# A fused attention and gated-FFN block: wv loaded in four row blocks on two queues, and tile 0's first v matmuls ahead of tile 2's transposes

## The chip, the cores and the metric

The kernel runs on one core of a Trainium2 chip. The metric is the device time of one execution in microseconds; the median of several executions is given. A core has five engines with an instruction stream each: TensorE (PE: matmuls, with the weight loads as PEld), VectorE (DVE), ScalarE (ACT), GpSimd (POOL) and SyncE (SP), which here only issues DMAs. ScalarE can issue DMAs too. An engine's stream is worked through in order, and engines wait for one another and for DMAs through semaphores.

## The reference

The input x has 2048 rows (tokens) of 512. It is normalized, and the output is x plus a linear attention of the result plus a gated FFN of it:

```python
qkv = (x @ wqkv) -> q, k, v              # 32 heads of 16
pq, pk = q @ w_phi, k @ w_phi            # per head
phi = concat(softmax(p), softmax(-p))    # for q and for k
kv, z = phi_k^T v, sum(phi_k)            # over all tokens, per head
o = (phi_q kv) / (phi_q z + 1e-6)
A = o @ wo
B = ((x @ w_gate) * (x @ w_up)) @ w_down # 512 -> 1792 -> 512
out = x + A(layernorm(x)) + B(layernorm(x))
```

All inputs are bf16. v takes the last 512 columns of wqkv; these are wv in the kernel, a 512 x 512 matrix.

## The kernel before

The 2048 tokens are 16 tiles of 128. TensorE contracts over partitions, so it needs the normalized x transposed: xnT holds, for each of the four 128-row blocks c of the 512 features, the 128 tokens of each tile. A projection of one tile into 512 columns is four matmuls of 512 columns, one for each block c, that add up in one bank of PSUM (`proj`); matmul j reads block j of xnT and row block j of the weights.

The instruction order of all five engines is written out by hand (`manual_schedule`): what stands first in the program text for an engine runs first on it. The SyncE DMAs at the top come in the order of the text too.

At the start of the program tiles 0 to 3 of x are treated apart, so that TensorE has work early:

- x tiles 0 and 2 are loaded by SyncE's queue, x tiles 1 and 3 by ScalarE's (`dma_x`, L68 and L69). Behind its two x tiles SyncE's queue issues wv in two halves of two row blocks each (`dma_wv`, L74 to L76, called in L84 and L85), then the first columns of w_gate and w_up (`dma_gu`, L72), w_phi (L87), further columns, the transposed load of the k part of wqkv (wT, L89), and the rest of x and of the weights.
- ScalarE's first instruction is a small Exp (L101), which brings its function table in; then its two x loads, then the sum of tile 1 (L376, tile `junk`, whose accumulated output is `tots[1]`).
- VectorE sums tile 0 (`sum_of`, L373) and makes 512 x - sum of it in two halves (`sub_sum`, L337, tile xn), then does the same subtraction for tile 1, and then sum and subtraction for tile 2 and for tile 3. Scaling by 1/std comes later, since it can be applied to the result of the projection.
- TensorE transposes xn of each tile (`lt`, L202 to L206, four transposes of 128 x 128; tile 0 in two halves) and ScalarE copies the result from PSUM into xnT (L206).
- `first_v(n, js)` (L353) does those of the four v matmuls of tile n that are named in js. Tiles 0 and 1 accumulate into the two kv banks (shown as `kv` in the profile), tiles 2 and 3 into banks of the common pool (`pv`).
- Ahead of all this `warm_up` (L306) runs matmuls on constants, ten at first, and two more of 512 columns between the transposes of tile 1 and tile 2 (L383).

Behind it come the first three units of the FFN (`ffn(3)`, matmuls L274 and L278), the fold of w_phi into wk (`fold`, L217), which reads wT and `bd`, and then a long stretch in which FFN units, k, v and q projections and the attention alternate.

The order around the change, on TensorE: `lt(0)`, `lt(1)`, two warm-ups, `lt(2)`, blocks 0 and 1 of v of tiles 0, 1 and 2, `lt(3)`, blocks 2 and 3 of v of tiles 0, 1 and 2, all of v of tile 3, FFN.

Of the kernel before, what the change touches and what calls it, by code (L numbers as in the profile page):

```python
# [21 lines left out]
def kernel(  # L22
# [12 lines left out]
    nc = tc.nc  # L35
    P = 128
    S, D = A_x.shape[-2], A_x.shape[-1]
# [4 lines left out]
    DC = D // P  # L42
# [15 lines left out]
    wv = wpool.tile([P, DC, D], BF16)  # L58
# [9 lines left out]
    def dma_x(lo, hi, eng=nc.sync):  # L68
        eng.dma_start(out=xall[:, lo:hi, :], in_=x_view[:, lo:hi, :])  # L69
# [1 line left out]
    def dma_cols(eng, w, src, lo, hi, at=0):  # L71
        eng.dma_start(out=w[:, :, lo - at:hi - at], in_=src[:, lo:hi].rearrange("(c p) f -> p c f", p=P))  # L72

    def dma_wv(lo, hi):  # L74
        nc.sync.dma_start(out=wv[:, lo:hi, :],
                          in_=A_wqkv[lo * P:hi * P, 2 * D:3 * D].rearrange("(c p) f -> p c f", p=P))  # L76

    def dma_gu(lo, hi):
        dma_cols(nc.sync, wg, B_w_gate, lo, hi)
        dma_cols(nc.sync, wu, B_w_up, lo, hi)  # L80

    dma_x(0, 1)
    dma_x(2, 3)
    dma_wv(0, 2)  # L84
    dma_wv(2, DC)  # L85
    dma_gu(0, 2 * P)
    nc.sync.dma_start(out=wphi[:], in_=A_w_phi.rearrange("(c h) d f -> (h d) c f", c=DC))  # L87
    dma_gu(2 * P, 5 * P)
# [12 lines left out]
    nc.scalar.activation(out=first[:], in_=ones[:, 0:1], func=AF.Exp, scale=1.0)  # L101
    dma_x(1, 2, nc.scalar)
    dma_x(3, 4, nc.scalar)
    ident = consts.tile([P, P], BF16)
    make_identity(nc, ident[:])
    mhalf = consts.tile([P, GT], F32)
# [38 lines left out]
    def bank(name, dt=F32, n=TT):  # L145
        return ps_s.tile([P, n], dt, name=name, tag="s")
# [55 lines left out]
    def lt(n, lo=0, hi=DC):  # L202
        tp = bank("tp", BF16).rearrange("p (c t) -> p c t", c=DC)
        for c in range(lo, hi):
            nc.tensor.transpose(out=tp[:, c, :], in_=xns[n][:, c * P:(c + 1) * P], identity=ident[:])  # L205
        nc.scalar.copy(out=xnT[:, lo:hi, n * P:(n + 1) * P], in_=tp[:, lo:hi, :])  # L206
# [27 lines left out]
    def proj(ps, n, w, js=range(DC)):  # L234
        for j in js:
            nc.tensor.matmul(ps, lhsT=xnT[:, j, n * P:(n + 1) * P], rhs=w[:, j, :],  # L236
                             start=(j == 0), stop=(j == DC - 1))
# [68 lines left out]
    def warm_up(k, reps=DC):  # L306
        for _ in range(k):
            nc.tensor.matmul(warm[:, 0:reps * P], lhsT=ones,
                             rhs=nc.const_aps.tensor(1.0, [P, reps * P], BF16), start=True, stop=True)
# [4 lines left out]
    with tc.tile_pool(name="ps_k", bufs=1, space=PSUM) as ps_k:  # L314
# [38 lines left out]
        def first_v(n, js):  # L353
            if n not in vps:
                vps[n] = kvbank[n][:] if n < 2 else bank("pv")
            proj(vps[n], n, wv, js)
# [23 lines left out]
        lt(0, 0, 2)  # L380
        lt(0, 2, DC)
        lt(1)
        warm_up(2)  # L383
        for n in (2, 3):
            sum_of(n)
            sub_sum(n, tots[n])
        lt(2)
        for n in range(3):
            first_v(n, (0, 1))
        lt(3)  # L390
        first_v(0, (2, 3))
        first_v(1, (2, 3))
        first_v(2, (2, 3))
        for n in (2, 3, 0, 1):
            stats_of(n)
            scales_of(n, float(D))
# [125 lines left out]
```

## Time and profile before

| | |
|---|---|
| median of 3 runs | 221.38 us (221.12, 221.38, 221.43) |
| the profiled execution, its own time | 220.88 us |
| its span, first to last instruction | 219.1 us |
| granted TensorE clock, mean of the span | 1.000 |
| moved by DMA in the span | 19.91 MB, mean 91 GB/s |

In the profile, times are counted from the first instruction of the span. A page gives the busy time of each engine, the chain of work that ended last (followed back from the last instruction, at each step to what released it) and the costliest groups of instructions. The costliest here are the FFN's matmuls, the second of these rows for the other of its two weights:

```profile
L274 PE MATMUL g<-xnT,wg 128*128 128x512 bf16 x224 | 57.5, 379 | 0.0
L278 PE MATMUL u<-xnT,wu 128*128 128x512 bf16 x224 | 57.5, 379 | 0.0
```

The columns: line, engine, operation, output and inputs, shape, count; busy us in total and mean ns of one; idle time of the engine just before them. Matmuls are pipelined: one lasts 379 ns from its start to its end, and the next starts about 215 ns after it. In the first 16 us the timeline lists the instructions in order of time, with the idle time before each and what released it in square brackets. A row with a q behind the engine's name (SPq, ACTq) is the issue of a DMA; how long the transfer then takes to land stands in the view of the DMA issues, for example:

```profile
wv<-in_A_wqkv_dram SPq DMA_DIRECT2D x2, 256.0 KB, 4.2
xall<-in_A_x_dram ACTq DMA_DIRECT2D x2, 128.0 KB, 2.8
```

The last number is the median time from the start of the issue to the landing, in us.

### The profile page before, as it was taken

The page shows a single profiled execution, that of the slowest core. Times are in us where ns is not written, and L with a number is a line of the kernel's source. Part 1 is how long each engine was busy: PE and PEld are TensorE (multiplying, and loading weights), DVE is VectorE, ACT ScalarE, POOL GpSimd, SP SyncE. Part 2 cuts the span into 40 slices and gives each one's busy share as a digit, 9 for nine tenths or more (in the row PEclk, how much of TensorE's full clock was granted, in tenths as well). Part 3 has the DMA queues.
Part 4 walks back from the last instruction along what each step waited for, and adds up shares of the span by engine and source line. Part 5 has one row for each costly group of instructions (what it writes and reads, how often), then busy time and mean ns, then how long its engine had stood idle before and what let it go on. Part 6 is the DMA issues. An engine that isn't in the chain of part 4 may idle for free.

```text
span 219.1 us, 3493 instructions
## 1 busy us (share of the span) xinstructions
PE 215.2 (98%) x1294; PEld 103.1 (47%) x1294; DVE 140.9 (64%) x239; ACT 89.4 (41%) x159; POOL 74.1 (34%) x71
## 2 busy tenths in 40 slices
PE   8999999999999999999999999999999999999994
PEld 3444445454444444444544444444444444454443
DVE  4868867886598758567599773296655645454321
ACT  5545686569574875565435212141231322100000
POOL 2450843363358454636045333033123033000000
PEclk9999999999999999999999999999999999999999
DMA  6999995303202540202018455114431431612301
GB/s 193 276 298 372 373 242 50 75 0 51 48 0 49 51 85 11 48 3 48 1 37 102 80 112 114 42 24 96 96 75 24 96 72 27 97 48 72 74 24 48
DMA packets 48529, 19.91 MB, mean 91 GB/s; under 512 B 37504, under 2 KB 48512, under 8 KB 48512
## 3 DMA queue, kind: packets, MB, share of 16 engines
q1 hardware_dynamic: 48224, 19.42, 39.8%
q10 hardware_dynamic: 288, 0.26, 0.4%
q8 instruction: 10, 0.16, 0.4%
q14 instruction: 7, 0.06, 0.1%
HBM read 8.67 MB, written 2.10 MB: 49 GB/s over the span
## 4 chain that ended last, share of the span: by engine, by line
PE 96%; DVE 1%; DMA 1%; issue 0%
PE g L274 22%; PE fin L290 22%; PE u L278 22%; PE fin L293 6%; PE k L236 6%; PE q L236 6%; PE pv L236 6%; PE ab L461 2%; PE kv L330 2%; DMA xall<-in_A_x_dram 1%; PE kv L236 1%; DVE tot L373 1%; PE pq L225 1%; DVE xn L337 0%; PE tp L205 0%
## 5 line engine op out<-in xcount | busy, mean ns | idle before, releaser
L274 PE MATMUL g<-xnT,wg 128*128 128x512 bf16 x224 | 57.5, 379 | 0.0
L278 PE MATMUL u<-xnT,wu 128*128 128x512 bf16 x224 | 57.5, 379 | 0.0
L282 DVE TENSOR_TENSOR hT<-u,g_sb 128x512 bf16<-128x512 f32 x56 | 37.0, 666 | 24.4 <-PE u L278 16.2
L253 POOL TENSOR_TENSOR phiq<-e,rsum 128x1024 bf16<-128x1024 f32 x16 | 30.9, 1933 | 63.5 <-DVE rsum L251 56.0
L281 ACT CAST g_sb<-g 128x512 bf16<-128x512 f32 x56 | 32.8, 586 | 47.1 <-PE g L274 46.9
L249 DVE TENSOR_REDUCE sums<-e 128x64 f32<-128x1024 f32 x32 | 38.9, 1216 | 20.1 <-ACT e L246 20.1
L290 PE MATMUL fin<-wd,hT 128*128 128x512 bf16 (+2 forms) x238 | 51.2, 367 | 0.0
L253 POOL TENSOR_TENSOR phik<-e,rsum 128x1024 bf16<-128x1024 f32 x16 | 30.9, 1932 | 40.0 <-DVE rsum L251 37.9
L278 PEld LDWEIGHTS <-wu 128*128 128x128 bf16 x224 | 21.9, 98 | 26.4
L290 PEld LDWEIGHTS <-hT 128*128 128x128 bf16 x238 | 22.4, 98 | 24.8
L274 PEld LDWEIGHTS <-wg 128*128 128x128 bf16 x224 | 21.1, 98 | 24.0
L236 PEld LDWEIGHTS <-xnT 128*128 128x128 bf16 x192 | 17.5, 97 | 18.3 <-ACT xnT L206 0.3
L300 DVE TENSOR_TENSOR o_sb<-fin,xall 128x512 bf16<-128x512 f32 (+2 forms) x13 | 8.5, 651 | 20.5 <-PE fin L293 20.5
L251 DVE RECIPROCAL rsum<-sums 128x64 f32<-128x64 f32 x32 | 17.7, 553 | 3.1
L293 PE MATMUL fin<-wo,oT 128*128 128x512 bf16 (+2 forms) x68 | 16.6, 367 | 0.0
L236 PE MATMUL k<-W1k,xnT 128*128 128x512 bf16 x64 | 16.4, 379 | 0.0
L236 PE MATMUL q<-W1q,xnT 128*128 128x512 bf16 x64 | 16.4, 378 | 0.0
L245 ACT ACTIVATE e<-q 128x512 f32<-128x512 f32 x12 | 7.2, 597 | 22.2 <-PE q L236 22.2
L236 PE MATMUL pv<-wv,xnT 128*128 128x512 bf16 x56 | 14.4, 380 | 0.0
L474 DVE TENSOR_TENSOR otok<-ab,rden 128x512 bf16<-128x512 f32 x16 | 11.1, 691 | 0.6
L322 ACT CAST vt<-pv 128x512 bf16<-128x512 f32 x12 | 7.0, 587 | 10.0 <-PE pv L236 10.0
L153 DVE BATCH_NORM_STATS2 stats<-xall 128x6 f32<-128x512 bf16 x16 | 10.6, 664 | 0.0
(61 smaller groups left out, 130.9 us busy)
## 6 DMA issues: line engine op xcount, KB each, us to landing
out_dram<-o_sb SPq DMA_DIRECT2D x15, 128.0 KB, 2.0
wd<-in_B_w_down_dram SPq DMA_DIRECT2D x1, 1792.0 KB, 15.4
xall<-in_A_x_dram SPq DMA_DIRECT2D x1, 1024.0 KB, 11.4
wg<-in_B_w_gate_dram SPq DMA_DIRECT2D x1, 640.0 KB, 7.7
wu<-in_B_w_up_dram SPq DMA_DIRECT2D x1, 640.0 KB, 9.5
wv<-in_A_wqkv_dram SPq DMA_DIRECT2D x2, 256.0 KB, 4.2
xall<-in_A_x_dram SPq DMA_DIRECT2D x1, 512.0 KB, 4.2
wg<-in_B_w_gate_dram SPq DMA_DIRECT2D x1, 512.0 KB, 5.3
```

Source lines behind the costliest of these rows:

```text
L153: nc.vector.bn_stats(out=stats[:], in_=xall[:, n, :])
L236: nc.tensor.matmul(ps, lhsT=xnT[:, j, n * P:(n + 1) * P], rhs=w[:, j, :], start=(j == 0), stop=(j == DC - 1))
L249: nc.vector.tensor_reduce(out=sums[:], in_=ev, axis=AX.X, op=ALU.add)
L251: nc.vector.reciprocal(out=rsum[:].rearrange("p a b -> p (a b)"), in_=sums[:])
L253: nc.gpsimd.tensor_tensor(out=phi[:].rearrange("p g (x f) -> p (g x) f", f=DH), in0=ev, in1=rsum[:].to_broadcast((P, 2 * H, DH)), op=ALU.mult)
L274: nc.tensor.matmul(gps, lhsT=wg[:, c, f * P:(f + 1) * P], rhs=xnT[:, c, T * TT:(T + 1) * TT], start=(c == 0), stop=(c == DC - 1))
L278: nc.tensor.matmul(ups, lhsT=wu[:, c, f * P:(f + 1) * P], rhs=xnT[:, c, T * TT:(T + 1) * TT], start=(c == 0), stop=(c == DC - 1))
L281: nc.scalar.copy(out=g_sb[:], in_=gps)
L282: nc.vector.tensor_tensor(out=hTs[T][:, f, :], in0=ups, in1=g_sb[:], op=ALU.mult)
L290: nc.tensor.matmul(ps, lhsT=hTs[T][:, f, t4 * P:(t4 + 1) * P], rhs=wd[:, f, lo:lo + w], start=(f == 0), stop=False)
L293: nc.tensor.matmul(ps, lhsT=oTs[n][:, c, :], rhs=wo[:, c, lo:lo + w], start=False, stop=(c == DC - 1))
L474: nc.vector.tensor_tensor(out=o_tok[:].rearrange("p (b h d) -> p b h d", b=2, d=DH), in0=abv[:, :, :, 0:DH], in1=rden[:].to_broadcast((P, ...
```

## The change

wv is loaded in four row blocks of 128 x 512 (128 KB each) instead of two halves: blocks 0 and 2 by SyncE's queue, in the place of the two halves, and blocks 1 and 3 by ScalarE's queue behind its x tiles, in the program text ahead of the sum of tile 1. On TensorE the two warm-ups behind `lt(1)` have 128 columns instead of 512; blocks 0 and 1 of v of tile 0 come ahead of `lt(2)`; behind `lt(2)` come blocks 0 and 1 of tile 1 and blocks 2 and 3 of tiles 0 and 1, then `lt(3)`, then all four blocks of tile 2. The number of matmuls of v, and what they compute, stays as it was.

```diff
-    def dma_wv(lo, hi):
-        nc.sync.dma_start(out=wv[:, lo:hi, :],
-                          in_=A_wqkv[lo * P:hi * P, 2 * D:3 * D].rearrange("(c p) f -> p c f", p=P))
+    def dma_wv(c, eng):
+        eng.dma_start(out=wv[:, c, :], in_=A_wqkv[c * P:(c + 1) * P, 2 * D:3 * D])
...
     dma_x(0, 1)
     dma_x(2, 3)
-    dma_wv(0, 2)
-    dma_wv(2, DC)
+    dma_wv(0, nc.sync)
+    dma_wv(2, nc.sync)
     dma_gu(0, 2 * P)
...
     nc.scalar.activation(out=first[:], in_=ones[:, 0:1], func=AF.Exp, scale=1.0)
     dma_x(1, 2, nc.scalar)
     dma_x(3, 4, nc.scalar)
+    dma_wv(1, nc.scalar)
+    dma_wv(3, nc.scalar)
...
         lt(1)
-        warm_up(2)
+        warm_up(2, 1)
+        first_v(0, (0, 1))
         for n in (2, 3):
             sum_of(n)
             sub_sum(n, tots[n])
         lt(2)
-        for n in range(3):
-            first_v(n, (0, 1))
+        first_v(1, (0, 1))
+        for n in range(2):
+            first_v(n, (2, 3))
         lt(3)
-        first_v(0, (2, 3))
-        first_v(1, (2, 3))
-        first_v(2, (2, 3))
+        first_v(2, range(DC))
```

## The prediction

> **What bounds the kernel now.** I read the page first, then the chain of waits over the first 18 us, then the timeline of the same stretch, the DMA issues one by one, and the queue's own waits.
>
> The page, span and chain:
>
> ```profile
> PE 215.2 (98%) x1294; PEld 103.1 (47%) x1294; DVE 140.9 (64%) x239; ACT 89.4 (41%) x159; POOL 74.1 (34%) x71
> ...
> PE 96%; DVE 1%; DMA 1%; issue 0%
> ```
>
> TensorE is busy almost throughout, and the chain that ends last is TensorE's. The remaining 4% lies mostly ahead of its first real stretch, which the chain shows in order of time (start, duration, what):
>
> ```profile
> 0.79 2.48 DMA xall<-in_A_x_dram
> ...
> 3.29 0.70 DVE tot L373
> ...
> 4.22 0.55 DVE xn L337 x2
> 4.76 0.60 DVE tot L373
> ...
> 5.39 0.37 DVE xn L337
> ...
> 5.80 0.40 PE tp L205 x4
> 6.20 0.86 PE kv L236 x4
> ```
>
> The reader is to see that tile 2's transposes, `lt(2)`, start at 5.80 because VectorE delivers xn of tile 2 at 5.75, and that from there on the chain is TensorE alone. In the timeline the first FFN matmul (g, L274) starts at 9.71. The work between is 16 wv matmuls at 0.215 us spacing, 3.44 us, and two groups of four transposes, 0.24 and 0.23 us: 3.91 us, which is exactly 9.71 - 5.80. So nothing waits after 5.80, and whatever the change does to 9.71 it does to the end, unless something later is late too.
>
> The timeline, the rows the change touches (start, duration, engine, line, operation):
>
> ```profile
> 0.84 0.86 ACTq L69 DMA_DIRECT2D xall<-in_A_x_dram  x2
> 1.71 0.94 SPq L75 DMA_DIRECT2D wv<-in_A_wqkv_dram  x2
> 3.45 0.63 ACT L376 ACTIVATE junk<-xall 128x512 bf16<-128x512 bf16 x1 [1.17 <-DMA xall<-in_A_x_dram]
> 3.99 0.19 ACT L376 ACTIVATION_READ_ACCUMULATOR junk<-xall 128x1 f32 x1
> 5.05 0.60 PE L308 MATMUL warm<-const-bfloat16-1.0 128*128 128x512 bf16 x2
> 5.77 0.54 SPq L72 DMA_DIRECT2D wu<-in_B_w_up_dram  x1
> ```
>
> ScalarE's sum of tile 1 (junk) starts as x tile 1 lands and gives tot of tile 1 at 4.18; VectorE uses it at 4.41, when it has finished tile 0. The slack is 0.23 us.
>
> The waits of SyncE's queue (waiting line, releaser: us, times, longest):
>
> ```profile
> SPq L72 <- DMA wv<-in_A_wqkv_dram: 0.6, 1, 0.6
> ```
>
> This row decides my forecast. A load of wu reads nothing of wv, yet its issue stood 0.6 us until wv had landed. The trace records a landing counter with each transfer, 103 to 110, eight in all, given out in turn over both queues: x0 103, x2 104, first wv 105, x1 106, second wv 107, x3 108, wg 109, wu 110, wphi 103 again, wg 104, wu 105. A transfer whose counter was used before is issued only when that earlier one has landed: the eleventh, this wu, waits for the third, wv, which landed at 1.71 + 4.0 = 5.71; the issue starts at 5.77.
>
> **The change, part by part.**
>
> Landings now, from each issue's start and its time to landing: x0 0.79 + 2.5 = 3.29; x1 0.84 + 2.6 = 3.44; x2 1.24 + 2.8 = 4.04; x3 1.25 + 3.1 = 4.35; wv blocks 0, 1 at 5.71; blocks 2, 3 at 2.18 + 4.3 = 6.48.
>
> *Order on TensorE.* Two warm-ups of 512 columns (0.215 each, 0.43) become two of 128 (four transposes of that width take 0.24, so about 0.06 each, 0.12): -0.31, in a stretch that waits for xn anyway, so nothing by itself. Two matmuls of tile 0 (0.43) move ahead of `lt(2)`. If wv has landed, 3.48 us instead of 3.91 are left behind `lt(2)`: -0.43, the most the change can bring. Behind `lt(2)` now stand six matmuls instead of four before its tile is read; behind `lt(3)` four instead of six: 0.86 us, the same distance that `lt(2)` has now, where the matmuls follow one another without a gap. Cost 0.
>
> *SyncE's queue.* Two issues of 0.43 and 0.47 remain two issues, with half the bytes; I take the same time. What shifts is the counters: with ten transfers where eight were, wphi would be the eleventh and wait for wv block 0 (about 5.2, worked out below) instead of going at 3.75. wg, wu and the transposed load of wT (issue 6.35, 4.38 long, landing 6.3 later at 12.65) then come 0.5 to 0.7 later. wT and bd are first read by the fold at 14.99, that wg by g at 13.17 (its landing 9.8 becomes about 11.3), so all stay hidden; uncovered it would cost what it is late, and none is.
>
> *ScalarE's queue.* Two issues more, 0.38 to 0.46 each as the two there are (0.86 together). Directly behind x3 they would run from 1.71 to 2.6, when ScalarE has nothing to do until 3.45: cost 0. But the counters count here as well. x1 and x3 came fourth and sixth in the common order, one ScalarE issue for each SyncE issue; going on like that, wv block 1 is the eighth, the last with a fresh counter, and wv block 3 the tenth, on the counter of x2. Its issue then stands until x2 lands at 4.04, and ScalarE's instructions are in order: junk is behind it. No row of before shows a waiting issue on ScalarE; the bound below is 0 (the issue is not held, or holds nobody), the bound above the full delay, and I take the latter, because on SyncE each next issue starts only after the waiting one (wu 5.77 + 0.54, wT 6.35).
>
> The Trainium skill says the same of the place of such a wait (DMA: Bandwidth & Descriptors, "Anatomy of one DMA"): "any semaphore wait happens on the issuing sequencer before dispatch"; the wu row agrees, for SyncE.
>
> The delay: x2 lands at 3.99 to 4.04 (the same record in two roundings); the issue starts 0.01 to 0.06 later; it lasts 0.38 to 0.46; junk starts 0.02 to 0.04 after it: 4.40 to 4.60. Its sum is there 0.73 later (3.45 to 4.18): 5.13 to 5.33. VectorE takes it up 0.03 to 0.06 on (xnT copied at 6.82, weights loaded at 6.88): 5.16 to 5.38 in place of 4.41, so 0.75 to 0.97 late. Everything behind it on VectorE is late by the same: tot and xn of tile 2, so `lt(2)` at 6.55 to 6.77, tile 3, the four statistics. TensorE has done tile 0's two matmuls by then: xnT of tile 0 is copied at about 5.7 behind junk, wv 0 and 1 have landed by 5.71, and xn (0.35) and transposes (0.24) of tile 1, the warm-ups (0.12) and these matmuls (0.43) end 1.14 after VectorE takes up tile 1, while `lt(2)` comes 1.39 after it (4.41 to 5.80). So 3.48 us are left: the first g at 10.03 to 10.25 in place of 9.71, +0.32 to +0.54. I take +0.46, a little above the middle, as the later issues on both queues were the longer ones.
>
> Late next: wv block 3, issued near 4.05 into an empty ScalarE queue; x3, the slowest such transfer, took 3.1, so 7.15 at the latest, and is read at about 6.7 + 0.24 + 0.43 + 0.22 = 7.5. VectorE's statistics, 0.9 late, move bd from 13.59 to about 14.5 and hT from 11.93 to about 12.8; the fold at 14.99 + 0.46 needs both later than that. Cost 0.
>
> *Moving wv faster over two queues.* In the windows, with both queues at work and with one (us; busy per engine, clock, DMA share, GB/s):
>
> ```profile
> 3.00:3.50 0.50, 0.50 (x3) 0.21 (x2) 0.21 (x1) 0.05 (x1) 0.00 (x0) 1.00 1.07 371
> 3.50:4.00 0.50, 0.50 (x5) 0.23 (x2) 0.48 (x1) 0.50 (x2) 0.00 (x0) 1.00 0.96 293
> 4.00:4.50 0.50, 0.42 (x5) 0.13 (x3) 0.48 (x3) 0.17 (x2) 0.00 (x0) 1.00 0.93 297
> 5.00:5.50 0.50, 0.50 (x6) 0.15 (x3) 0.47 (x2) 0.50 (x3) 0.00 (x0) 1.00 0.91 290
> ```
>
> 332 GB/s against 294, so wv 0 and 1 may land earlier than 5.71. Extending the x tiles (x2 is 0.75 behind x0, x3 0.91 behind x1) gives 4.79 and 5.26 for blocks 0 and 1; the bound above is 5.71. In my forecast this is hidden behind VectorE; it sizes the rival.
>
> The Trainium skill speaks against a gain here (DMA: Bandwidth & Descriptors, "Issuing engines are not separate DMA queues"): queues share the DMA engines, and issuing from several saves issue time only. By it wv 0 and 1 land at 5.71 as now and the rival below gains 0.05; by the rows, up to 0.43.
>
> **The sum.** 220.88 us of the profiled execution (219.1 span, 1.8 around it) + 0.46 = 221.34. The median of the runs is 0.50 above that execution, so 221.84 against 221.38; by the bounds alone 221.70 to 221.92.
>
> **The rivals.**
> A, no issue of ScalarE is held (the four wv issues all get fresh counters): junk stays at 3.45, `lt(2)` at 5.80. Tile 0's matmuls start at 5.30 (full gain, 0.43) to 5.75 (5.75 + 3.91 = 9.66, gain 0.05). 220.95 to 221.33, middle 221.1. For it: ScalarE is idle from 2.29 to 3.45. Against: ten transfers by the tenth issue and eight counters. It decides from the point where the wait ends before 3.2, as junk has 0.23 us of slack.
> B, wv block 3 is the ninth and waits for x0 (3.29): issue to 3.75, junk 3.78, tot at 4.51, VectorE 0.14 late, `lt(2)` at 5.94, g at 9.42 at best and 9.66 at worst: 221.1 to 221.35. For it: the order between queues hangs on hundredths. Against: the strict alternation above.
> C, the delay is longer: the held issue takes 0.88, as the wg issue at 4.30 on SyncE did when much was queued, or wv block 3 lands like the wv halves (4.3 after issue, 8.35, read at 7.5: 0.85 on top). +0.9 to +1.3: 222.3 to 222.7. For it: these rows. Against: ScalarE's queue is nearly empty by then.
>
> **Chances.** Forecast 0.60, A 0.17, B 0.08, C 0.15. A measurement of this kernel tells about 0.2%, 0.44 us, from no change. Of the forecast's bounds some five parts of eight lie above +0.44: slower 0.60 x 0.63 + 0.14 = 0.52. Faster: half of A and a fifth of B, 0.11. Within: the rest, 0.37. The forecast's own range is 221.65 to 222.0; to leave out no more than 2 in 10 the range reaches over most of A and B and the near end of C: 221.05 to 222.35.
>
> **What would show it.** Right: a fourth ScalarE issue at 4.0 to 4.1, junk at 4.4 to 4.6, VectorE idle some 0.8 us before xn of tile 1, `lt(2)` at 6.55 to 6.77 with tile 0's wv matmuls ahead of it, first g near 10.15, wphi issued after 5. Wrong: that issue at about 2.2 and junk at 3.45 (A), or a wv matmul of tile 0 that waits behind `lt(2)` (C).

## The result: slower by 0.7%

| | median us | executions | ratio to before, 95% interval |
|---|---|---|---|
| before | 221.28 | 6 (220.93 to 221.43) | |
| changed | 222.83 | 6 (222.28 to 223.27) | 1.0070 [1.0053, 1.0088] |

The change costs 1.55 us at the median. The forecast, 221.84 within 221.05 to 222.35, had the sign but not the size: 222.83 lies above its range. The profiled execution of the changed kernel took 223.27 us, 2.39 more than the profiled one of before; its span is 221.5, 2.4 more.

The page of the changed kernel, busy time of each engine:

```profile
PE 215.6 (97%) x1270; PEld 104.0 (47%) x1294; DVE 141.1 (64%) x239; ACT 89.4 (40%) x159; POOL 74.1 (33%) x71
```

TensorE's busy time hardly moved, but the trace has records of only 1270 of its 1294 matmuls, so this sum does not tell where the time went; the starts of the matmuls do. The first FFN matmul (g) starts at 12.03 instead of 9.71: 2.32 of the 2.4 us are lost before it. The chain of waits over that stretch (start, duration, what):

```profile
1.25 2.89 DMA xall<-in_A_x_dram
...
4.16 0.33 ACTq L75
...
4.54 0.73 ACT junk L377 x2
...
5.30 0.36 DVE xn L338
...
6.53 0.96 PE kv L237 x2
7.49 0.43 PE tp L206 x4
7.92 2.32 PE kv L237 x6
10.24 0.22 PE tp L206 x4
10.46 1.73 PE pv L237 x8
```

The upper half is the forecast's mechanism: x tile 2 lands at 4.14, only then does ScalarE's fourth issue go, and junk and VectorE's xn of tile 1 follow it. The lower half is not: the two matmuls of tile 0 take 0.96 and the six that follow 2.32, 0.39 each and more, where 0.215 was counted on; the last eight are back at 0.215. The timeline (start, duration, engine, line, operation, and the idle time with its releaser) shows the same events with their waits:

```profile
1.75 0.45 ACTq L75 DMA_DIRECT2D wv<-in_A_wqkv_dram  x1
...
4.54 0.63 ACT L377 ACTIVATE junk<-xall 128x512 bf16<-128x512 bf16 x1 [2.26 <-DMA xall<-in_A_x_dram]
5.30 0.35 DVE L338 TENSOR_SCALAR xn<-xall,tot 128x512 bf16<-128x512 bf16 x1 [0.98 <-ACT junk L377]
...
6.46 0.37 SPq L86 DMA_DIRECT2D wphi<-in_A_w_phi_dram  x1
```

wv block 1 is issued at once, at 1.75; block 3 stands 2 us, from 2.20 to 4.16. The profile puts junk's wait down to its data, x tile 1, but that had landed at 3.35: it was the issue ahead of it. wphi waits for wv block 0, as forecast, for longer (block 0 landed at 6.44). The trace records sixteen increments for each transfer, and the last is its landing. In that execution this gives 6.44, 6.65, 6.88 for blocks 0 to 2, and 8.9 for block 3, 4.7 after its issue.

The weight loads of TensorE in the same stretch:

```profile
8.14 0.15 PEld L237 LDWEIGHTS <-xnT 128*128 128x128 bf16 x1 [0.28 <-issue]
8.57 0.15 PEld L237 LDWEIGHTS <-xnT 128*128 128x128 bf16 x1 [0.28 <-issue]
```

They come every 0.43 us (two more follow at 9.00 and 9.42) and last 0.15 instead of about 0.10, as those of the very first warm-ups do: TensorE's clock was at half speed until 9.85. (The clock row of the page shows nine tenths and more there, since its record begins only with the first rise.) In the profiled execution of before the rise was at 4.1.

So three suspects: the held issue, block 3's late landing, which the slow matmuls may hide, and the clock.

### The profile page after: what moved, and what is told of

Same layout as the page of the kernel before. It is cut to its first block, busy times and chain, and to the rows that moved or that the text cites. A ratio compares the mean times of both kernels' runs of the same rounds, so it can differ in the third digit from the quotient of the medians.

```text
span 221.5 us, 3471 instructions
## 1 busy us (share of the span) xinstructions
PE 215.6 (97%) x1270; PEld 104.0 (47%) x1294; DVE 141.1 (64%) x239; ACT 89.4 (40%) x159; POOL 74.1 (33%) x71
## 4 chain that ended last, share of the span: by engine, by line
PE 96%; DMA 1%; issue 1%; ACT 0%; DVE 0%; SPq 0%; ACTq 0%
PE g L275 22%; PE u L279 22%; PE fin L291 22%; PE fin L294 6%; PE q L237 6%; PE k L237 6%; PE pv L237 5%; PE ab L462 2%; PE kv L331 2%; PE kv L237 1%; DMA xall<-in_A_x_dram 1%; PE tp L206 1%; PE pq L226 1%; ACT junk L377 0%; SPq L69 0%
## 5 line engine op out<-in xcount | busy, mean ns | idle before, releaser
L275 PE MATMUL g<-xnT,wg 128*128 128x512 bf16 x215 | 56.5, 379 | 0.5
L279 PE MATMUL u<-xnT,wu 128*128 128x512 bf16 x220 | 56.8, 379 | 0.2
L237 PE MATMUL k<-W1k,xnT 128*128 128x512 bf16 x60 | 15.7, 379 | 0.1
```

What stands on the lines that cost most here:

```text
L275: nc.tensor.matmul(gps, lhsT=wg[:, c, f * P:(f + 1) * P], rhs=xnT[:, c, T * TT:(T + 1) * TT], start=(c == 0), stop=(c == DC - 1))
L279: nc.tensor.matmul(ups, lhsT=wu[:, c, f * P:(f + 1) * P], rhs=xnT[:, c, T * TT:(T + 1) * TT], start=(c == 0), stop=(c == DC - 1))
```

## The experiments

Ratios are those of each run against the kernel before on the same chip; where executions scatter in two groups they differ from the quotient of the medians.

| run | median us | before us | ratio, 95% interval |
|---|---|---|---|
| e1_loads_alone | 222.66 | 221.05 | 1.0081 [1.0057, 1.0105] |
| e2_order_alone | 221.22 | 221.05 | 1.0017 [0.9997, 1.0037] |
| e3_wv3_on_sync | 221.46 | 221.05 | 1.0041 [1.0014, 1.0068] |
| e4_fill | 222.33 | 221.05 | 1.0057 [1.0045, 1.0069] |
| e5_scalar_free | 222.47 | 220.97 | 1.0050 [1.0034, 1.0067] |
| e6_sync_warm | 221.34 | 220.97 | 1.0014 [1.0003, 1.0026] |
| e7_wu_behind | 221.62 | 220.97 | 1.0024 [1.0014, 1.0033] |
| e8_wv_ahead | 221.09 | 220.97 | 0.9996 [0.9983, 1.0008] |
| e9_wv_ahead_bare | 220.79 | 221.22 | 0.9985 [0.9973, 0.9997] |
| e10_loads_ahead_old_order | 221.32 | 221.22 | 1.0011 [0.9996, 1.0026] |
| e11_look | 223.0, one execution | 221.22 | |

### The loads alone

The changed kernel with TensorE's order and warm-ups of before:

```diff
-        warm_up(2, 1)
-        first_v(0, (0, 1))
+        warm_up(2)
...
-        first_v(1, (0, 1))
-        for n in range(2):
-            first_v(n, (2, 3))
+        for n in range(3):
+            first_v(n, (0, 1))
         lt(3)
-        first_v(2, range(DC))
+        first_v(0, (2, 3))
+        first_v(1, (2, 3))
+        first_v(2, (2, 3))
```

> The four loads of the change with TensorE's order and the two 512-column warm-ups of before. Held issue (wv block 3 on ScalarE's queue waits for x2, junk behind it): issue at 4.0 to 4.2, junk at 4.4 to 4.6, lt(2) at 6.6 to 6.8, then 3.91 us: first g at 10.5 to 10.7, +0.8 to +1.0 us. Late landing (wv block 3 is served behind wg and wu and lands at 7.3 or later): in this order it is read only at about 8.4, so it adds no more than 0.5. Clock: if the short warm-ups are what keeps TensorE slow in the changed kernel, its matmuls here are at 0.215 us spacing from 6.5 on; if not, 0.43 us spacing shows here too.

Measured: issue at 4.02, junk at 4.40, `lt(2)` at 6.55, first g at 10.46 in the profiled execution (221.7 us), 0.75 after that of before. That is the held issue by itself: block 3 landed at 8.03, and in this order it is read only at about 8.5. But the six executions fall in two groups, 221.70 to 222.10 and 223.22 to 223.59, a spread of 1.9 us that neither landing nor hold explains. The profiled one, of the first group, ran at full clock by 5.6. The two long warm-ups are in this run, but behind tile 1's transposes; the hold leaves TensorE idle ahead of them, from 4.9 to 5.6. Whether the slow group is the clock is not shown, since no execution of that group was profiled.

### The order alone

The kernel before with TensorE's order of the change:

```diff
-        warm_up(2)
+        warm_up(2, 1)
+        first_v(0, (0, 1))
...
         lt(2)
-        for n in range(3):
-            first_v(n, (0, 1))
+        first_v(1, (0, 1))
+        for n in range(2):
+            first_v(n, (2, 3))
         lt(3)
-        first_v(0, (2, 3))
-        first_v(1, (2, 3))
-        first_v(2, (2, 3))
+        first_v(2, range(DC))
```

> TensorE's order and the short warm-ups of the change with the two wv halves of before on SyncE's queue. Held issue or late landing as the cause: neither is here, junk at 3.45, lt(2) at 5.8 to 6.2, first g at 9.3 to 9.7, 0 to -0.4 us. Clock as the cause: matmuls at 0.43 us spacing after 6 us and slower than before by 0.3 us or more.

Measured: no gain. Ten executions lie between 220.92 and 221.39, two at 222.91 and 223.24, the latter with a mean granted clock of 0.992. In the profiled one wv's first half landed at 6.25, and TensorE waited for it ahead of `lt(2)`:

```profile
6.29 0.59 PE L236 MATMUL kv<-wv,xnT 128*128 128x512 bf16 x2 [0.58 <-DMA wv<-in_A_wqkv_dram]
6.72 0.38 PE L205 MATMUL tp<-ident,xn 128*128 128x128 bf16 x4
```

The reader is to see that `lt(2)`, ready at 5.8, now stands behind a wait for wv: when wv is later than xn of tile 2, the new order puts tile 2's four transposes, 0.24 us, behind that wait; in the old order they stand ahead of it.

### Block 3 on SyncE's queue

The changed kernel with one transfer moved:

```diff
     dma_wv(2, nc.sync)
+    dma_wv(3, nc.sync)
...
     dma_wv(1, nc.scalar)
-    dma_wv(3, nc.scalar)
```

> The change with one transfer moved: wv block 3 is third on SyncE's queue instead of second on ScalarE's, so that it is the eighth transfer at the latest. No transfer on ScalarE's queue is held, and wv block 3 goes ahead of wg and wu. Held issue and late landing as the causes: junk at 3.45, all of wv landed by 6.6, first g at 9.3 to 9.7, 0 to -0.4 us against the kernel before. Clock as the cause: still slower than before by 0.3 us or more, with 0.43 us spacing.

Measured: junk at 3.58, nothing held on ScalarE, all of wv landed by 7.04, first g at 10.20. With the held issue and block 3's late landing gone, most of the loss is gone in seven of the twelve executions: 220.50 to 221.49. There is no gain even so, because `lt(2)` starts only at 6.73: tile 0's matmuls ahead of it waited 0.85 us for wv block 0, which landed at 6.26. The other five took 222.13 to 223.50, and one of these has a mean granted clock of 0.992: 0.008 of its 221.8 us span is 1.8 us lost, which is 3.5 us at half clock. This points to the clock as a cause of its own that strikes in a share of the executions; a profile of such an execution follows below.

### TensorE kept busy

The changed kernel with three more warm-ups in the idle time:

```diff
         lt(0, 2, DC)
+        warm_up(3)
         lt(1)
```

> The change with three more warm-up matmuls of 512 columns between the transposes of tile 0 and of tile 1, where TensorE stood idle from 4.8 to 5.7. Clock as a cause: matmuls after 6.5 at 0.215 us spacing, first g at about 11.5 instead of 12.03, 0.4 to 0.6 us faster than the changed kernel (222.3). Rival, the clock comes when it comes whatever is done there: 222.8 as the changed kernel. Late landing: even at full clock a matmul of tile 0 waits for wv block 3 until about 7.4 to 8.9.

Measured: 222.06 to 222.58 in five executions, a spread of 0.52 us where the changed kernel has 0.99 (222.28 to 223.27), and the matmuls are at 0.215 from 6.3 on, first g at 11.32. Against before it is 1.0057 where the changed kernel was 1.0070; the intervals overlap, so the clock's share of the median, some 0.3 us, is not clear of the noise. What it uncovers is plain:

```profile
7.04 0.82 PE L237 MATMUL kv<-wv,xnT 128*128 128x512 bf16 x3
8.73 0.81 PE L237 MATMUL kv<-wv,xnT 128*128 128x512 bf16 x3 [0.86 <-DMA wv<-in_A_wqkv_dram]
```

After three matmuls TensorE waits 0.86 us for wv block 3, which landed at 8.68, 4.6 after its issue.

### ScalarE not held

The changed kernel with block 3 issued behind junk, and the 512-column warm-ups:

```diff
-    dma_wv(3, nc.scalar)
...
         nc.scalar.activation(out=junk[:], in_=xall[:, 1, :], func=AF.Identity, accum_out=tots[1][:])
+        dma_wv(3, nc.scalar)
...
-        warm_up(2, 1)
+        warm_up(2)
```

> The change with the fourth issue of ScalarE's queue (wv block 3) put behind the sum of tile 1, so that it holds nobody, and with the two 512-column warm-ups of before, so that TensorE's clock stays out of it. Held issue as the only cause: junk at 3.45 to 3.6, lt(2) at 5.8 to 6.7 as wv blocks 0 and 1 land, 221.0 to 221.4. Late landing as the larger cause: wv block 3, issued at about 3.6 behind wg and wu, still lands at 7.5 to 8.7, TensorE waits for it in the middle of tile 0, first g at 10.4 to 11.3, 221.9 to 222.5.

Measured: junk at 3.44 and not held; the issue itself went at 3.44, 0.6 earlier than in the run before. And yet:

```profile
6.19 0.59 PE L236 MATMUL kv<-wv,xnT 128*128 128x512 bf16 x2 [0.67 <-DMA wv<-in_A_wqkv_dram]
...
6.84 0.81 PE L236 MATMUL kv<-wv,xnT 128*128 128x512 bf16 x3
8.67 0.81 PE L236 MATMUL kv<-wv,xnT 128*128 128x512 bf16 x3 [1.01 <-DMA wv<-in_A_wqkv_dram]
```

Block 3 landed at 8.63 again, and the first g starts at 11.27 against 11.32. Taking the hold away gains next to nothing, for two reasons. Ahead of `lt(2)`, tile 0's matmuls wait 0.67 us for wv block 0 (landed at 6.15), so that `lt(2)` starts at 6.62, against 6.75 in the run before, with the hold. Behind it, the wait for block 3 is there as before. Four executions took 222.45 to 222.65 and two 221.73 and 221.75; what the two had different is not shown. That an issue 0.6 earlier lands no earlier suggests that the transfer stands behind something else.

### The clock once more

The run with block 3 on SyncE's queue, with the warm-ups of before:

```diff
-        warm_up(2, 1)
+        warm_up(2)
```

> The run with wv block 3 on SyncE's queue, with the two 512-column warm-ups of before in place of the short ones. Clock: executions above 222 us, 5 of 12 without the warm-ups, are gone or at most one; the median is 221.0 to 221.4. Rival, something else than the clock makes those executions slow: they stay at about 5 of 12. No gain over before is expected, as wv blocks 0 and 1 landed at 6.3 to 6.5 in that run.

Measured: eleven of twelve executions at 220.73 to 221.71, one at 222.14. With the two longer warm-ups nearly all of the executions above 222 are gone. Five of twelve against one of twelve is a small count; it fits that the kernel before, with the same two warm-ups, had none above 221.92 in the 81 executions of all comparisons here. The run stays 0.14% above before, with a first g at 9.93 and wv blocks 0 and 1 landing at 5.98 and 6.21, for which TensorE again waits ahead of `lt(2)`.

The run with the short warm-ups again, nothing edited:

> One more look at the run with wv block 3 on SyncE's queue and the short warm-ups, of which 5 of 12 executions took over 222 us. If the profiled one is such an execution: by the clock theory its v matmuls, or those of the first FFN unit, follow one another at 0.43 us for up to 3.4 us, and its mean clock is below 1 or its weight loads last 0.15 instead of 0.10. If it is one of the others it tells nothing new.

The profiled execution is of that kind, 223.0 us, with wv blocks 0 and 1 landed at 6.09 and 6.32:

```profile
6.13 1.01 PE L237 MATMUL kv<-wv,xnT 128*128 128x512 bf16 x2 [0.36 <-DMA wv<-in_A_wqkv_dram]
6.94 0.63 PE L206 MATMUL tp<-ident,xn 128*128 128x128 bf16 x4
7.37 2.60 PE L237 MATMUL kv<-wv,xnT 128*128 128x512 bf16 x6
9.81 0.39 PE L206 MATMUL tp<-ident,xn 128*128 128x128 bf16 x4
10.03 1.89 PE L237 MATMUL pv<-wv,xnT 128*128 128x512 bf16 x8
```

Six matmuls over 2.44 us (7.37 to 9.81), then eight over 1.73: the clock rose at about 9.7, and the first g started at 11.76 instead of 10.20, 1.56 later with nearly the same landings (6.26 and 6.46 there). One kernel, two executions, and the clock rose at 4.9 in the one and at 9.7 in the other.

### What block 3 stands behind

The run with three more warm-ups, with one issue moved: the first wu columns behind wphi on SyncE's queue, so that they are issued after block 3.

```diff
-    dma_gu(0, 2 * P)
+    dma_cols(nc.sync, wg, B_w_gate, 0, 2 * P)
     nc.sync.dma_start(out=wphi[:], in_=A_w_phi.rearrange("(c h) d f -> (h d) c f", c=DC))
+    dma_cols(nc.sync, wu, B_w_up, 0, 2 * P)
```

> The run with three more warm-ups (222.33), with one issue moved: the first 256 columns of wu go behind wphi on SyncE's queue, so that they are issued behind wv block 3 and not ahead of it. If transfers of both queues are served in the order of their issue, wv block 3 lands 0.6 to 0.9 earlier (7.6 to 8.1 instead of 8.68), TensorE's wait for it shrinks by as much, 221.5 to 221.9. Rival, ScalarE's queue itself is slow or gets a small share: landing and time as they were, 222.3.

Measured: block 3 landed at 7.77 instead of 8.68, 0.91 earlier, at the same issue time (4.08 against 4.04); TensorE's wait for it shrank from 0.86 to 0.15, first g at 10.41. 1.0024 [1.0014, 1.0033] against 1.0057 [1.0045, 1.0069]: the place of one SyncE issue, ahead of or behind a transfer of ScalarE's queue, is worth about 0.7 us of the kernel's time. The times carry this, since no execution of the one run reaches into the range of the other (221.22 to 221.87 and 222.06 to 222.58). The landing alone would not: with the same issues ahead of it block 3 landed at 8.03 in the run with the loads alone and at 8.91 in the changed kernel. So what SyncE's queue issued earlier delays a transfer on ScalarE's queue. The records of the changed kernel's landings agree: by the median increment x0, x1, x2, x3, wv 0, 1, 2, wg, wu, wv 3 come in just that order, 2.84 to 7.31, and wv 3's packets come mostly after 6, two microseconds behind its issue. The order is not strict: in the run with ScalarE not held, wu was issued 0.28 ahead of block 3 and landed at 8.87, block 3 at 8.63. The view of the DMA queues of the changed kernel from 5.5 to 6.0 us and from 6.5 to 7.0 shows where the time went, with SyncE's queue (q1) and ScalarE's (q10):

```profile
q1 hardware_dynamic: 305, 0.15, 102.2%
q10 hardware_dynamic: 6, 0.01, 3.5%
...
q10 hardware_dynamic: 78, 0.07, 46.7%
q1 hardware_dynamic: 86, 0.04, 28.1%
```

The columns are packets, MB and share of 16 engines. Block 3 had been issued at 4.16. In this trace the first packets of x tiles 0 and 1, with little ahead of them, came 1.0 and 1.3 us after their issues; up to 6.0, 1.8 us after its own, block 3 has almost none, while SyncE's queue has the engines nearly to itself with wg and wu, issued at 2.65 and 3.13.

The Trainium skill has the DMA engines taking turns between the queues that have work, packet by packet (DMA: Bandwidth & Descriptors, "Queues, rings and completion order"). The second pair of rows agrees, as both queues are served in one stretch, block 3 with 46.7% and SyncE's queue with 28.1%. The delay lies ahead of that, in when block 3's packets come; whether they are made only then or wait somewhere is not shown. Nor does moving wu tell a place in line from the mere amount of traffic: it takes wu's 256 KB out of that stretch altogether.

### A version with the order of issues turned to use

wv in the two halves of before, the first on ScalarE's queue between its two x tiles, the second on SyncE's; TensorE's order of the change with one 512-column warm-up. The diff is against the kernel before and leaves out the lines of that order behind `lt(2)` and the new `dma_wv`:

```diff
-    dma_wv(0, 2)
-    dma_wv(2, DC)
+    dma_wv(2, DC, nc.sync)
...
     dma_x(1, 2, nc.scalar)
+    dma_wv(0, 2, nc.scalar)
     dma_x(3, 4, nc.scalar)
...
         lt(1)
-        warm_up(2)
+        warm_up(1)
+        first_v(0, (0, 1))
```

> A candidate: wv in the two halves of before, the first on ScalarE's queue between its two x tiles (third or fourth of all issues), the second on SyncE's behind x tile 2; TensorE's order of the change with one 512-column warm-up. Order of issue: the first half lands about 0.4 earlier than in the kernel before (5.2 to 5.8), x tile 3 about 0.8 later, which VectorE needs only at 5.7; no issue is held. 220.7 to 221.1, 0 to -0.4 us. Rival, wv lands no earlier or tile 3 becomes late: 221.2 to 221.6.

Measured: the first half landed at 4.64, 1.1 before that of the kernel before and more than expected, x tile 3 at 6.32. 0.9996: no difference. In the profiled execution the clock rose only at about 6.5, so the warm-up (0.43) and tile 0's two matmuls (0.43 each) put `lt(2)` at 6.46. Without that warm-up:

```diff
         lt(1)
-        warm_up(1)
         first_v(0, (0, 1))
```

> The candidate with the first wv half ahead of x tile 3, without any warm-up behind lt(1): tile 0's v matmuls start as soon as xnT of tile 0 is there, at about 5.25, since the half had landed at 4.64. At full clock lt(2) starts at 5.8, first g at 9.3 to 9.4: 220.5 to 220.7. Where the clock rises only at about 6.5, these two matmuls take 0.86 and lt(2) starts at 6.1: 220.8 to 221.1. Median 220.6 to 220.9 against 221.0 of before. Rival, the missing warm-up lets the clock rise later still: executions above 222.

Measured: 220.79 against 221.22, 0.9985 [0.9973, 0.9997], and no execution above 221.5. It is faster than the kernel before by some 0.3 us and has the lowest ratio here; its interval ends just below 1 and overlaps that of the run with the warm-up.

```profile
5.26 0.60 PE L236 MATMUL kv<-wv,xnT 128*128 128x512 bf16 x2
5.85 0.40 PE L205 MATMUL tp<-ident,xn 128*128 128x128 bf16 x4
6.08 0.59 PE L236 MATMUL kv<-wv,xnT 128*128 128x512 bf16 x2
6.85 1.02 PE L236 MATMUL kv<-wv,xnT 128*128 128x512 bf16 x4 [0.17 <-DMA wv<-in_A_wqkv_dram]
```

Tile 0's matmuls now lie in the time before xn of tile 2 is ready, as the change meant them to; the wait has moved to the second half of wv (landed at 6.81). First g at 9.66.

And these loads with TensorE's order and warm-ups of before:

```diff
-        first_v(0, (0, 1))
+        warm_up(2)
...
         lt(2)
-        first_v(1, (0, 1))
-        for n in range(2):
-            first_v(n, (2, 3))
+        for n in range(3):
+            first_v(n, (0, 1))
         lt(3)
-        first_v(2, range(DC))
+        first_v(0, (2, 3))
+        first_v(1, (2, 3))
+        first_v(2, (2, 3))
```

> The same loads with TensorE's order and the two warm-ups of before. If the order pays once wv is there early, this one is slower than the run with the new order by 0.2 to 0.4. If only the wait for wv counted, it is as fast: lt(2) at 5.8, no wait for wv behind it, 0 to -0.2 us against before.

Measured: 1.0011 [0.9996, 1.0026] against 0.9985 [0.9973, 0.9997] for the new order without warm-up. It has two groups as well, 220.83 to 221.41 and 221.88 to 222.23. In the profiled execution, of the second group, x tile 3 landed at 7.37 and `lt(3)` waited for it until 8.52. So with these loads the new order is the better one by about 0.5 us at the median, though the intervals just touch and the two runs differ in the warm-ups as well. The late tile 3 is the price of these loads in the profiled execution; that it makes the whole second group is not shown.

## Why the prediction was wrong, point by point

**The counters and the held issue: right.** Block 1 went at 1.75 with a fresh counter, block 3 at 4.16 (4.0 to 4.1 forecast), junk at 4.54 (4.40 to 4.60), VectorE took up tile 1 at 5.30 (5.16 to 5.38), and xn of tile 2 was there at 6.63. The loads alone moved the first g by 0.75, the lower end of the 0.75 to 0.97 that this step gave for VectorE.

**"Late next: wv block 3 ... 7.15 at the latest": the step that failed.** It was priced from x tile 3, which took 3.1 from issue to landing, on the ground that ScalarE's queue was empty. An empty queue was not the point: the transfer came behind wg and wu, issued 1.5 and 1.0 us before it on the other queue, and took 4.6 to 4.7. The run that moved wu behind it is what shows this. The cost of this term, set at 0, is about 0.7 us between the two runs that differ in this issue alone. The rival C had this landing as its second row (4.3 after the issue, 8.35) and a time near the measured one, 222.3 to 222.7; it was given 0.15 because of the same "nearly empty" queue.

With wu moved and TensorE kept busy, the forecast's own case is what is left: 1.0024 is 0.53 us over before, where +0.46 was forecast, and the first g starts at 10.41, where 10.15 was forecast. From there the first g goes to 11.32 with wu ahead of block 3 (1.26 us over before, by the ratio) and to 12.03 in the changed kernel, where the clock is low as well (1.55).

**TensorE at full clock throughout: the second term that was missing.** All terms used 0.215 us for each matmul. In the changed kernel TensorE idles between 4.8 and 5.7 us and has two short warm-ups instead of two long ones, and its clock stayed low until 9.85 in the profiled execution. Two runs bear the cause out: longer warm-ups took the executions over 222 us from 5 of 12 to 1 of 12, and the profiled one of that kind has its matmuls at 0.43 until 9.8. I wrote of the two long warm-ups that removing them was "nothing by itself"; where nothing is held, they were the cover. Where the hold makes TensorE idle they may not be enough: the loads alone, with both long warm-ups, had three of six executions above 223. In the changed kernel itself the clock and the late landing overlap, and its own share, about 0.3 us, is not settled.

The Trainium skill puts the rise of the clock down to a free-running window of about 3.4 us in which TensorE has to be busy (TensorE: Matmul & The Clock Gate, Part 1). That fits: one kernel had its rise at 4.9 in one execution and at 9.7 in another, 3.5 us of half clock come out of the 0.992 above, and the executions scatter in groups.

**"wv 0 and 1 have landed by 5.71": too early, and hidden behind the hold.** From the rows I put blocks 0 and 1 at 4.79 to 5.71. In seven of the eight profiled executions with four blocks they landed between 5.98 and 6.65, in one at 5.50 and 5.69. The new order puts tile 0's matmuls, and so this landing, ahead of `lt(2)`: in the four runs that hold nothing on ScalarE and have the new order with wv behind the x tiles, `lt(2)` starts at 6.46 to 6.73 at full clock, much as in the run with the loads alone, where the hold puts it at 6.55. So the hold and the landing of wv each put `lt(2)` at about the same time, and that the hold's size came out right does not make it the only limit there.

**wv over two queues: no gain, as the Trainium skill's rule had it.** Even with nothing held and the longer warm-ups, the four blocks were at 1.0014, not below 1, so rival A's gain was not there either. A half of wv issued on ScalarE's queue at 1.25 instead of 1.71 landed 1.1 earlier, more than the 0.46 of issue time: it had passed x tile 3.

**Sums.** Of the forecast's bounds, +0.32 to +0.54, less than half lies above +0.44, not five parts of eight; with that, "slower" had a chance of 0.41 instead of 0.52. The time at which block 3 is read adds up to 7.59, not 7.5, and wv block 0 stands at 5.2 in one place and at 4.79 in another. None of this decides the outcome.

**What was taken as hidden: right.** bd was ready at 14.5 as forecast and the fold began without a wait for it; wphi's issue at 6.46 and wT's landing at 13.77 held up nothing.

## What to carry to other kernels

Count the transfers in flight before adding one: with a fixed ring of landing counters, a transfer too many waits for an earlier one's landing, and all that stands behind it on the issuing engine waits with it. Judge when a load will land by what is issued ahead of it on all queues, not by whether its own queue looks empty. And before taking out a warm-up whose result nobody reads, look for whether the engine still stays busy without it, and look at the scatter of several executions, not at one profile. Work that is put ahead of a step that is ready makes that step wait for the work's own inputs.

## What the runs showed of the hardware that was not expected

By their median increments, the first ten transfers of the changed kernel landed in the order in which they were issued over both queues, SyncE's and ScalarE's. Moving one 256 KB issue of SyncE behind a 128 KB transfer of ScalarE brought that one 0.91 us forward and made the kernel about 0.7 faster; issuing the 128 KB transfer 0.6 us earlier, but still behind that issue, brought its landing 0.05 forward. Single landings scatter by as much as the first of these figures, so the effect rests on the kernel's time.

The clock can rise late: over the profiled executions, matmuls came to full speed between 3.6 and 9.9 us although all of them began with the same ten warm-ups at 0.8.

The same wv rows landed between 4.64 and 6.65 depending on their place among the first ten transfers, and between two executions of the same place they differ by up to 1.0. In the changed kernel the last of the sixteen increments of block 0 came 0.9 after the fifteenth (5.51 and 6.44), in others most of the sixteen were late. Why is open.
